# Top-k attention into a GELU block: in 18 slots POOL normalises P ahead of the next softmax's thresholds

## The chip, the core and the metric

The kernel runs on one core of a Trainium2 chip. A core has engines that work side by side, each through its own queue in order: TensorE (PE in the profile, with its weight loads as PEld), VectorE (DVE), ScalarE (ACT), GpSimd (POOL) and the queue that starts transfers (SP). An instruction that needs what another engine makes waits for a semaphore, and everything behind it in its queue waits too. The metric is the device time of one execution in microseconds.

## The reference

```python
# attention: q, k, v of (8 batches, 8 heads, 576 rows, 64)
scores = scale * np.matmul(q, k.transpose(0, 1, 3, 2))
kth = np.partition(scores, -top_k, axis=-1)[..., -top_k:-top_k + 1]   # top_k = 32
scores = np.where(scores >= kth, scores, -1e9)
attn = np.exp(scores - scores.max(axis=-1, keepdims=True))
attn = attn / (attn.sum(axis=-1, keepdims=True) + 1e-9)
attn_out = np.matmul(attn, v)
# bridge: (B,H,S,D) -> x of (4608 tokens, 512)
h = x @ w_in                                       # 512 x 2048
g = 0.5 * h * (1.0 + erf(h / sqrt(2)))
return g @ w_out                                   # 2048 x 512
```

All of it is in fp32. Each row of scores keeps its 32 largest values; the rest get no weight.

## The kernel before

**Items and slots.** The attention is cut into 144 items (`items`, `N`). A main item is one tile of 128 query rows for a pair of heads; its scores are one SBUF tile `s` of 128 x 1152, two rows of 576. A tail item collects the last 64 rows of two pairs. The main loop runs over slots `n` (0 to 147), and each slot holds one stage of each of several items: scores of item n+2, top-k of item n, softmax of item n-1, transposes of item n-2, and `attend` (P times v) of item n-3. Between those, `mlp` puts pieces of the GELU block on PE: first-layer matmuls (`l1_piece`, L673), second-layer products (`products`, L811 and L809; `even_piece`, L773 and L776). From slot 13 on the flag `few[0]` is set, and the order is that of the steady state. The schedule is manual: the order of the Python calls is the order in each engine's queue.

**What item n goes through.**

- `scores` and `last_keys`: PE makes the scores, ACT copies them scaled into `s` (L378, and L341 for the last key columns).
- `sum_up` (L413, POOL), `larger` (L406, DVE) and `smaller` (L421, POOL) split the 1152 columns of a "paired" item into lists of the larger and the smaller halves, of 128 x 576 each. `larger(n + 1)` stands at the head of slot n, and so right behind the end of `top_k(n - 1)` in DVE's queue. Items 0, 1 and 18 to 27 are not paired.
- `top_k` (DVE): rounds of MAX8 (L450) and MATCH_REPLACE8 (L453). Ahead of its very end stands `inverse(n - 1)`, the reciprocal `rden` (L482) of the previous item's softmax sum. Then come a small maximum of two lists (L465) and a reduction (L466), which give the 32nd largest value `kth`.
- `threshold` (POOL): `neg` = -kth (L475) and `bias` = kth - maximum (L476), both of 128 x 2.
- `softmax` (ACT, in the next slot, one call for each of the two rows): a steep Prelu with `neg` (L495), which pushes down everything below kth, and an Exp with `bias` (L496), whose sum is `den`. `add_small` (POOL, L488) adds 1e-9.
- `normalise` (POOL): s times rden over 128 x 1152 (L507).
- `transposes`: PE turns the normalised P: `tails`, the last columns (L527; behind two matmuls L333 that make score columns of another item), and `turn_both`, eight 128 x 128 transposes (L553). ACT copies both out (L537, L574).
- `attend`: PE multiplies by v (L615, tail items L626). ACT copies the result into `xT` (L620, L631), the input of the GELU block.

So POOL's queue at the end of slot n is `threshold(n)`, `normalise(n - 1)`, `sum_up(n + 2)`, then whatever small sums of the GELU block are due (`run_small`). DVE's queue is the end of `top_k(n)`: reciprocal of item n-1, L465, L466; then slot n+1's `larger(n + 2)`.

**Chunks.** The GELU block works on chunks of 256 tokens (or 128 for the collected tails). A chunk can start once all heads of its tokens have gone through `attend`. In the slot where `attend` finishes a chunk, PE often has no piece of the GELU block left that may run ahead of it. The loop then puts the transposes of item n-2 first (`turned`, then `tails`), and the pieces of the fresh chunk behind them:

```python
if product and n > START and done[0] < len(pieces) and pieces[done[0]][0] > ready[0]:
    if turned:
        turned()
    for piece in tr[:1]:
        piece(n + 2 if few[0] else None)
    tr, ready[0] = tr[1:], n_tok[0]
```

In every other slot pieces of the block stand ahead of the transposes.

Of the kernel before, what the change touches and what calls it, by code (L numbers as in the profile page):

```python
# [14 lines left out]
def kernel(  # L15
# [30 lines left out]
    NP = H // 2  # L46
    NM = S // P
# [151 lines left out]
    def weights_size(u):  # L199


        if u not in words:
            return
        w, first, below, d = parts(u)
        nc.scalar.activation(below, first, func=AF.Prelu, bias=high, scale=2.0**-40, alpha=2.0**40)
        nc.scalar.activation(d, below, func=AF.Prelu, bias=low, scale=2.0**59, alpha=2.0**-40)
        if on_dve(u):
            nc.vector.tensor_scalar(
                w.bitcast(i32), w.bitcast(u32), 2.0**-13, None, op0=ALU.mult
            )  # L210
        else:
            nc.scalar.activation(w.bitcast(i32), w.bitcast(u32), func=AF.Copy, scale=2.0**-13)
# [5 lines left out]
    def waits(u):  # L218

        return u == ORDER[-1]  # L220
# [3 lines left out]
    def weights_add(u):  # L224
        if u in words:
            w, _, _, d = parts(u)
            nc.gpsimd.tensor_tensor(d, d, w.bitcast(i32), op=ALU.add)
        made.add(u)


    items, starts = [], []
# [14 lines left out]
    N = len(items)  # L246
# [4 lines left out]
    few = [False]  # L251
# [106 lines left out]
    def scores(i, second=False):  # L358
        if i >= N or i in S_of:
            return  # L360
        pair, t = items[i]
        S_of[i] = s = work.tile([P, 2 * S], f32, tag="s", bufs=6, name="s")
        s_ps = pair_tile("s_ps", "l1" if second else "pr")
        if not few[0]:
            last_keys(i, bank("t_ps"))()
        if t < NM:
            q_t, kt = q_of[pair][:, t * P : (t + 1) * P], kt_of[pair]
            for e in range(2):
                rows = slice(e * D, (e + 1) * D)
                nc.tensor.matmul(  # L370
                    s_ps[:, e], lhsT=q_t[rows, :], rhs=kt[rows, 0:SM], start=True, stop=True
                )
            if i == 0:

                nc.scalar.activation(s[:, 0:SM], s_ps[:, 0], func=AF.Copy, scale=scale)
                nc.scalar.activation(s[:, S + TL :], s_ps[:, 1], func=AF.Copy, scale=scale)  # L376
                return
            nc.scalar.activation(spread(s, S + TL, SM), s_ps, func=AF.Copy, scale=scale)  # L378
        else:

            for r in range(2):
                kt = kt_of[pair + r]
                for e in range(2):
                    rows = slice(e * D, (e + 1) * D)
                    nc.tensor.matmul(
                        s_ps[half(r, e), r, :], lhsT=kt[rows, SM + P + e * TL : SM + P + (e + 1) * TL],
                        rhs=kt[rows, 0:SM], start=True, stop=True,
                    )
            s2 = s.rearrange("p (r n) -> p r n", r=2)
            nc.scalar.activation(s2[:, :, 0:SM], s_ps, func=AF.Copy, scale=scale)  # L390
# [12 lines left out]
    def larger(i):  # L403

        if paired(i):
            nc.vector.tensor_tensor(lists_of[i][:, 0], *halves_of(i), op=ALU.max)  # L406
# [63 lines left out]
    def threshold(i):  # L470

        if i < 0 or i >= N:
            return
        st = stat_of[i]
        nc.gpsimd.tensor_scalar(st["neg"], st["kth"], -1.0, None, op0=ALU.mult)  # L475
        nc.gpsimd.tensor_tensor(st["bias"], st["kth"], st["first"][:, :, 0], op=ALU.subtract)  # L476
# [13 lines left out]
    def softmax(i, e):  # L490

        if i < 0 or i >= N:
            return
        st, s = stat_of[i], row(i, e)
        nc.scalar.activation(s, s, func=AF.Prelu, bias=st["neg"][:, e : e + 1], scale=1.0, alpha=STEEP)  # L495
        nc.scalar.activation(  # L496
            s, s, func=AF.Exp, bias=st["bias"][:, e : e + 1], scale=1.0,
            accum_out=st["den"][:, e : e + 1],
        )

    def normalise(i):

        if i < 0 or i >= N:
            return
        s, r = S_of[i].rearrange("p (e n) -> p e n", e=2), stat_of[i]["rden"]
        wide = bass.AP(tensor=r.tensor, offset=r.offset, ap=[list(r.ap[0]), [1, 2], [0, S]])
        nc.gpsimd.tensor_tensor(s, s, wide, op=ALU.mult)  # L507
# [5 lines left out]
    def transposes(i):  # L513
# [43 lines left out]
        def main(e):  # L557
            tp = bank("tp")
            turn_over(tp, e)
            nc.scalar.copy(  # L560
                out=pt_now[0][:, e * NM : (e + 1) * NM, x : x + P],
                in_=tp.rearrange("p (j n) -> p j n", j=NM),
            )
# [16 lines left out]
            return [tails, lambda _: both(), turn_both]  # L580
        return [tails] + [lambda _, e=e: main(e) for e in range(2)]

    def copy_x():
        while copies:
            copies.pop()()
# [387 lines left out]
    def room_in(n):  # L973

        x = n - START - 1
        if x < 1:
            return 4
        if x >= len(sizes):
            return 0
        return sizes[x] + (1 if x % 2 == 0 else -1)  # L980
# [38 lines left out]
    for pair in range(2, n_pairs):  # L1019
        b, p = divmod(pair, NP)  # L1020
# [9 lines left out]
    for n in range(ahead):  # L1030

        left[0] = room_in(n)
        few[0] = n > START + 2
        eager[0] = n > N
        if not waits(unit_in(n)):
            weights_add(unit_in(n))
        larger(n + 1)
        for piece in squares_in.pop(n, []):
            piece()
        two = few[0] and n % 2 == 0 and n + 3 < N and items[n + 3][1] < NM  # L1040
        scores(n + 2, two)
        if two:
            scores(n + 3)
        product = attend(n - 3)
        late = n > START
        if n <= START:

            softmax(n - 1, 0)
        copy_x()
        if waits(unit_in(n)):  # L1050
            weights_size(unit_in(n))
            weights_add(unit_in(n))
        mlp(1)
        if few[0] and n % 2:
            run_gelus()
        tr = transposes(n - 2)
        turned = tr.pop() if few[0] and tr else None
# [7 lines that stand above are left out]
        if not few[0] and n > START:  # L1065
            softmax(n - 1, 0)
        mlp(1)
        if not late:
            softmax(n - 1, 1)
        if few[0]:  # L1070
            softmax(n - 1, 0)
            if n % 2:
                mlp(ODD)
        mlp(1)
        if n < START:

            keep_busy((4 if product or n == 0 else 14) * (1 if n < 5 else 2), ident)
        prep = prep_in.pop(n, [])
        if n == START + 1:

            for piece in prep:
                piece(None)
            prep = []
        if len(prep) > 1 and len(tr) == 3:
            tr, prep = tr[:1] + prep[:1] + tr[1:], prep[1:]
        now = tr[:-1]
        if few[0]:
            now, tr, prep = tr + prep[:1], [], prep[1:]
        for x, piece in enumerate(now):
            piece(n + 2 if few[0] else None)  # L1090
            if n < START and product and x == 0:
                keep_busy(5 if n < 5 else 10, ident)
            ready[0] = n_tok[0]
            if few[0] and x == 2:
                break
            mlp(1)
        ready[0] = n_tok[0]
        if late:
            softmax(n - 1, 1)
        smaller(n + 1)  # L1100
        add_small(n - 1)
        for piece in tr[-1:] + prep:
            piece(None)
            mlp(1)
        if n == 1:
            keep_busy(8, ident)

        run_gelus()
        mlp(left[0])
        run_gelus()  # L1110
        if n < N:
            top_k(n, lambda: inverse(n - 1))
        else:
            inverse(n - 1)
        threshold(n)
        normalise(n - 1)
        sum_up(n + 2)
        if n in sums_in:
            weight_sums(sums_in[n])
        run_small(6)  # L1120

        if not waits(unit_in(n + 1)):
            weights_size(unit_in(n + 1))
        for m in (n + 1, n + 2):

            if m > 2 and waits(unit_in(m)) == (m == n + 1):
                load_weights(m)
        if n < NP:
            load("v", n)
# [38 lines left out]
```

## Time and profile before

| what | us |
|---|---|
| median of 3 runs | 1556.66 (1553.4 to 1557.61) |
| profiled execution, time | 1557.3 |
| profiled execution, span | 1555.5 |
| PE busy | 1522.8 |
| DVE busy | 1330.3 |
| ACT busy | 1165.3 |
| POOL busy | 1141.5 |

The granted TensorE clock was 0.994 over the span. Rows of the profile give start, duration, engine, line, operation, what it writes and reads, and in brackets the idle time of the engine ahead of it with what ended it. Where several instructions of one line follow each other they are merged into one row with their count. The answer for one line gives the least, median and greatest duration in ns, and "who waited for it" the idle time of others that its end released, with the number of times.

### The profile page before, as it was taken

What the parts mean: (1) busy time and instruction counts of PE and PEld (TensorE: products, weight loads), DVE (VectorE), ACT (ScalarE), POOL (GpSimd) and SP (SyncE); (2) the same over time, 40 slices, a digit from 0 to 9 for tenths busy, and PEclk for the clock granted to TensorE, in tenths of its full rate; (3) what the DMA queues carried; (4) which work ended last, traced back from release to release, by engine and by line L of the source; (5) the groups of instructions that cost most, each with busy time, mean ns of one, the idle gap of its engine ahead of it and who ended that gap; (6) DMA issues with size and microseconds to landing.
All of it is one profiled execution on the core that took longest, in us unless ns stands there. A gap on an engine that the chain in (4) does not pass through costs nothing. (4 is left out here: it accounts for less than half of the span.)

```text
span 1555.5 us, 28139 instructions
## 1 busy us (share of the span) xinstructions
PE 1522.8 (98%) x9280; PEld 1199.5 (77%) x9280; DVE 1330.3 (86%) x4571; ACT 1165.3 (75%) x2050; POOL 1141.5 (73%) x1291
## 2 busy tenths in 40 slices
PE   7899999999999999999999999999999999999998
PEld 5676578877777778887777778787877777787887
DVE  8998799989999988998989997988998998988700
ACT  6998877767777777777777778777777777777720
POOL 4886567767787868777787877776788786877632
PEclk9999999999999999999999999999999999999999
DMA  6513210012101111012201111002110111000000
GB/s 180 158 61 117 89 45 1 1 37 54 24 15 31 35 26 31 1 30 42 39 18 16 30 31 45 1 23 36 34 24 22 24 30 32 15 1 15 7 14 14
DMA packets 185298, 56.35 MB, mean 36 GB/s; under 512 B 176161, under 2 KB 176705, under 8 KB 185153
## 3 DMA queue, kind: packets, MB, share of 16 engines
q1 hardware_dynamic: 183888, 54.13, 14.6%
q8 instruction: 73, 1.20, 0.3%
q14 instruction: 73, 0.59, 0.1%
q10 hardware_dynamic: 1200, 0.39, 0.1%
q0 software_dynamic: 64, 0.03, 0.0%
HBM read 45.08 MB, written 9.44 MB: 35 GB/s over the span
## 5 line engine op out<-in xcount | busy, mean ns | idle before, releaser
L673 PE MATMUL h_ps<-xT,w_in_sb 128*128 128x256 f32 (+1 forms) x2560 | 541.4, 362 | 1.9 <-ACT xT L620 1.9
L673 PEld LDWEIGHTS h_ps<-xT,w_in_sb 128*128 128x128 f32 x2560 | 435.4, 191 | 73.4 <-issue 25.3
L450 DVE MAX8 top<-lists 128x8 f32<-128x288 f32 x792 | 321.1, 447 | 0.0
L507 POOL TENSOR_TENSOR s<-s,rden 128x1152 f32<-128x1152 f32 x144 | 302.7, 2102 | 0.3 <-DVE rden L482 0.3
L496 ACT ACTIVATE s<-s,bias 128x576 f32<-128x576 f32 x288 | 223.3, 775 | 11.9
L453 DVE MATCH_REPLACE8 lists<-top,lists 128x288 f32<-128x288 f32 x528 | 229.8, 443 | 0.0
L495 ACT ACTIVATE s<-s,neg 128x576 f32<-128x576 f32 x288 | 225.7, 784 | 2.8 <-POOL neg L475 2.7
L450 DVE MAX8 low<-lists 128x8 f32<-128x288 f32 x528 | 213.1, 445 | 0.0
L574 ACT COPY pt<-tp 128x1024 f32<-128x1024 f32 x133 | 134.8, 1014 | 96.1 <-PE tp L553 96.1
L488 POOL TENSOR_SCALAR den<-den 128x2 f32<-128x2 f32 x144 | 31.4, 218 | 236.0 <-ACT s L496 232.1
L421 POOL TENSOR_TENSOR lists<-lists 128x576 int32<-128x576 int32 x132 | 186.3, 1411 | 4.0
L413 POOL TENSOR_TENSOR lists<-s 128x576 int32<-128x576 int32 x132 | 185.6, 1406 | 0.0
L553 PE MATMUL tp<-ident,s 128*128 128x128 f32 x1152 | 150.7, 274 | 7.7 <-POOL s L507 7.7
L553 PEld LDWEIGHTS tp<-ident,s 128*128 128x128 f32 x1152 | 133.7, 141 | 27.3 <-POOL s L507 14.0
L615 PE MATMUL o<-pt,raw_v 128*64 128x256 f32 x1280 | 154.1, 386 | 0.4 <-ACT pt L560 0.4
L615 PEld LDWEIGHTS o<-pt,raw_v 128*64 128x64 f32 x1280 | 86.9, 137 | 87.0 <-issue 44.7
L475 POOL TENSOR_SCALAR neg<-kth 128x2 f32<-128x2 f32 x132 | 85.6, 649 | 88.3 <-DVE kth L466 88.3
L482 DVE RECIPROCAL rden<-den 128x2 f32<-128x2 f32 x144 | 23.4, 162 | 139.8 <-POOL den L488 138.6
L811 PE MATMUL y_ps<-w_out_sb,sum 128*128 128x256 f32 x480 | 142.8, 379 | 0.0
L378 ACT ACTIVATE s<-s_ps 128x1024 f32<-128x1024 f32 x127 | 124.3, 1025 | 15.7 <-PE s_ps L370 15.5
L370 PE MATMUL s_ps<-kt,qm 64*128 64x512 f32 x512 | 131.2, 626 | 0.8 <-ACT s L376 0.8
L453 DVE MATCH_REPLACE8 lists<-low,lists 128x288 f32<-128x288 f32 x264 | 114.9, 443 | 0.0
(148 smaller groups left out, 2784.1 us busy)
## 6 DMA issues: line engine op xcount, KB each, us to landing
raw_v<-in_v_dram SPq DMA_DIRECT2D x64, 128.0 KB, 2.4
out_dram<-y SPq DMA_DIRECT2D x30, 256.0 KB, 2.1
w_out_sb<-in_moe_w_in_dram SPq DMA_DIRECT2D x14, 511.8 KB, 4.9
raw_q<-in_q_dram SPq DMA_DIRECT2D x96, 64.0 KB, 2.0
raw_k<-in_k_dram SPq DMA_DIRECT2D x96, 64.0 KB, 2.0
w_out_sb<-in_moe_w_out_dram SPq DMA_DIRECT2D x10, 511.8 KB, 4.1
w_sum<-in_moe_w_out_dram SPq DMA_DIRECT2D x6, 511.8 KB, 4.1
raw_q<-in_q_dram SPq DMA_DIRECT2D x96, 8.0 KB, 1.8
```

The costliest lines, as they stand in the source:

```text
L413: nc.gpsimd.tensor_tensor(t[:, 1].bitcast(i32), a.bitcast(i32), b.bitcast(i32), op=ALU.add)
L421: nc.gpsimd.tensor_tensor(both, both, top, op=ALU.subtract)
L450: nc.vector.max(x[:, e], src[:, e])
L453: nc.vector.match_replace(dst[:, e], x[:, e], src[:, e], LOWEST)
L495: nc.scalar.activation(s, s, func=AF.Prelu, bias=st["neg"][:, e : e + 1], scale=1.0, alpha=STEEP)
L496: nc.scalar.activation(s, s, func=AF.Exp, bias=st["bias"][:, e : e + 1], scale=1.0, accum_out=st["den"][:, e : e + 1],)
L507: nc.gpsimd.tensor_tensor(s, s, wide, op=ALU.mult)
L553: nc.tensor.transpose(tp[:, j * P : (j + 1) * P], s[:, first + j * P : first + (j + 1) * P], ident)
L574: nc.scalar.copy(out=pt_now[0][:, 0 : 2 * NM, x : x + P], in_=tp.rearrange("p e (j n) -> p (e j) n", j=NM),)
L615: nc.tensor.matmul(o[e * D : (e + 1) * D, 0:n], lhsT=vt[:, j, e, :], rhs=pt[:, e * NM + j if j < NM else 2 * NM, :], start=(j == 0), stop= ...
L673: nc.tensor.matmul(h_tile(u)[:, i, :], lhsT=w_in_sb[:, ko, f * P : (f + 1) * P], rhs=xT[:, ko, c0 : c0 + n], start=(ko == 0), stop=(ko == ...
L811: nc.tensor.matmul(acc[names][:, k], lhsT=lhsT, rhs=rhs, start=(j == 0 and k == 0), stop=(j == FT // 2 - 1 and k == 1),)
```

## The change

A helper `closes(i)` says whether `attend` of item i finishes a chunk: the last pair of heads in a batch with an odd tile, or the second of the two tail items of an odd batch. In slot n, if item n-2 is such an item (its `attend` comes in slot n+1), the two calls at the end of the slot change places: `normalise(n - 1)` goes on POOL's queue first, `threshold(n)` behind it. In all other slots nothing changes.

```diff
+    def closes(i):
+        if i < 0 or i >= N:
+            return False
+        pair, t = items[i]
+        b, at = divmod(pair, NP)
+        return at == NP - 1 and t % 2 == 1 if t < NM else at == NP - 2 and b % 2 == 1
...
-        threshold(n)
-        normalise(n - 1)
+        if few[0] and closes(n - 2):
+            normalise(n - 1)
+            threshold(n)
+        else:
+            threshold(n)
+            normalise(n - 1)
         sum_up(n + 2)
```

The slots are 17, 21, 29, 37, 45, 53, 57, 65, 73, 81, 89, 93, 101, 109, 117, 125, 129 and 137; 145 is selected as well, but there is neither a threshold nor a further item in it. In 21, 57, 93 and 129 the chunk finished is one of 128 tail tokens.

## The prediction

> **What bounds the kernel now.** I read the page's busy shares first, then the answer for the line that normalises P (L507), then the timeline around the slots the change touches, engine by engine.
>
> ```profile
> PE 1522.8 (98%) x9280; PEld 1199.5 (77%) x9280; DVE 1330.3 (86%) x4571; ACT 1165.3 (75%) x2050; POOL 1141.5 (73%) x1291
> ...
> L507 POOL TENSOR_TENSOR s<-s,rden x144: 2097/2102/2108, 30.5 to 1479.4; 128x1152 f32<-128x1152 f32 x144
> ...
>   PE tp L553: 7.7, 13
> ...
>   PE tp_t L527: 0.5, 3
> ```
>
> PE is busy 98% of the span, so only its gaps can be won. The row of L553, under "who waited for it", is the prize: in 13 places PE's large transposes (L553) waited for the normalised P, 7.7 us together. No edit of this kind can bring more than that, 0.5% of the span. One place, slot 45 and what follows it, row by row:
>
> ```profile
> 478.15 0.15 DVE L482 RECIPROCAL rden<-den 128x2 f32<-128x2 f32 x1
> 478.27 0.19 DVE L465 TENSOR_TENSOR top<-top,low 128x32 f32<-128x32 f32 x1
> 478.60 0.75 DVE L406 TENSOR_TENSOR lists<-s 128x576 f32<-128x576 f32 x1
> 478.76 0.66 POOL L475 TENSOR_SCALAR neg<-kth 128x2 f32<-128x2 f32 x1 [1.20 <-DVE kth L466]
> 479.54 2.10 POOL L507 TENSOR_TENSOR s<-s,rden 128x1152 f32<-128x1152 f32 x1
> 481.69 1.09 PE L553 MATMUL tp<-ident,s 128*128 128x128 f32 x8 [1.09 <-POOL s L507]
> 488.27 0.17 DVE L482 RECIPROCAL rden<-den 128x2 f32<-128x2 f32 x1 [0.40 <-POOL den L488]
> 489.61 2.10 POOL L507 TENSOR_TENSOR s<-s,rden 128x1152 f32<-128x1152 f32 x1
> 493.54 0.27 PE L527 MATMUL tp_t<-ident,s 128*128 128x128 f32 x1
> ```
>
> The reciprocal that L507 needs is ready at 478.30, but POOL first waits for kth, makes neg and bias, and starts L507 at 479.54. It ends at 481.64 and PE, idle for 1.09, starts 0.05 later.
>
> **The change part by part.** No instruction is added or removed on any engine; PE, DVE, ACT and SP keep their order. In POOL's queue L507 moves ahead of L475 and L476 in 18 slots: 17, 21, 29, 37, 45, 53, 57, 65, 73, 81, 89, 93, 101, 109, 117, 125, 129 and 137 (slot 145 is chosen too, but has no threshold). So it stops waiting for kth and queues only behind the reciprocal.
>
> *What L507 gains.* In slot 45 POOL started 0.08 after the reduce of kth ended (the row of neg), so I start L507 0.08 after the reciprocal, at 478.38 instead of 479.54. That is 1.16 earlier, or 1.1 if the little maximum L465 holds it a moment. The largest of the 13 waits is 1.09, so all of them go: minus 7.7 us if nothing is late in exchange.
>
> *What neg and bias lose.* They now stand behind 2.10 us of L507, and end some 2 us later. The softmax on ACT waits for neg. In an ordinary closing slot ACT reaches that softmax only after copies that wait for the same transposes, so I cost this at nothing there; without that cover it would cost ACT up to 2 us a slot. In three slots (57, 93, 129; after the next fence) ACT goes straight to it, and is costed below. POOL's next operation, the sum L413, starts no later than now, since POOL no longer idles for kth.
>
> *What the early L507 meets.* Now it starts after the two-input maximum L406 of DVE has begun and soon finished; after the change it is in flight when L406 wants to start. The trace shows what such pairs do to POOL:
>
> ```profile
> L475 POOL TENSOR_SCALAR neg<-kth x132: 217/658/662, 38.6 to 1471.1; 128x2 f32<-128x2 f32 x132
> L475 POOL TENSOR_SCALAR neg<-top x12: 218/219/789, 19.3 to 297.5; 128x2 f32<-128x2 f32 x12
> ...
> 286.97 0.22 POOL L475 TENSOR_SCALAR neg<-top 128x2 f32<-128x2 f32 x1
> 287.01 0.76 DVE L406 TENSOR_TENSOR lists<-s 128x576 f32<-128x576 f32 x1
> 287.15 0.67 POOL L476 TENSOR_TENSOR bias<-top,first 128x2 f32<-128x2 f32 x1
> ```
>
> The same neg takes 0.22 us alone and 0.66 where it starts behind L406: in slot 45 it ends at 479.42, 0.07 after L406 (479.35). POOL is held until DVE's instruction is over. The bias at 287.15 shows it again, ending 0.05 after L406. The other order, POOL in flight and L406 coming, stands only once, at 286.97, with a neg of two columns, and neither was held. So how long L406 is held by a 2.10 us L507 is not shown. Its lower bound is 0 (that one row). Its upper bound is the rest of L507: 478.38 + 2.10 + 0.07 - 478.60 = 1.95, or 2.05 where L406 comes 0.39 instead of 0.45 after the reciprocal, as it does in most slots. I take 2.05: the rows nearest in kind, where two long readers really overlap, all show the second held to the end of the first, while the lone neg reads two columns and may have read them before L406 asked. The Trainium skill, "SBUF — State Buffer", section "Who interferes with whom", says that a VectorE instruction with two SBUF inputs and a GpSimd instruction that reads SBUF exclude each other, whoever starts first having the port for its whole instruction; the trace agrees for VectorE first, and by the rule the hold here would be those 2 us, by the lone row nothing.
>
> *What 2.05 us on DVE costs.* L406 heads the next item's top-k, so DVE's reciprocal one slot later is late by 2.05 less the time it already waits there. L507 of that slot (not swapped) is late by as much, and PE reads it first with the small transpose L527, two slots on. In slot 45's case: 2.05 - 0.40 = 1.65 late; L507 ended 491.71 and PE came at 493.54, a margin of 1.78 after the 0.05 hand-over. The net is margin minus lateness, 0.13 won of 1.09; the other 0.96 is a new wait of PE. Slots 81 and 117 repeat slot 45: 3 x 0.13 = 0.39. The other families:
>
> ```profile
> 197.50 1.09 PE L553 MATMUL tp<-ident,s 128*128 128x128 f32 x8 [0.22 <-POOL s L507]
> ...
> 327.20 0.17 DVE L482 RECIPROCAL rden<-den 128x2 f32<-128x2 f32 x1
> 328.53 2.10 POOL L507 TENSOR_TENSOR s<-s,rden 128x1152 f32<-128x1152 f32 x1
> 332.72 0.27 PE L527 MATMUL tp_t<-ident,s 128*128 128x128 f32 x1
> ...
> 407.99 0.17 DVE L482 RECIPROCAL rden<-den 128x2 f32<-128x2 f32 x1 [0.46 <-POOL den L488]
> 409.32 2.10 POOL L507 TENSOR_TENSOR s<-s,rden 128x1152 f32<-128x1152 f32 x1
> 413.26 0.27 PE L527 MATMUL tp_t<-ident,s 128*128 128x128 f32 x1
> ...
> 563.25 1.09 PE L553 MATMUL tp<-ident,s 128*128 128x128 f32 x8 [0.49 <-POOL s L507]
> 570.07 0.17 DVE L482 RECIPROCAL rden<-den 128x2 f32<-128x2 f32 x1 [1.43 <-POOL den L488]
> 571.40 2.10 POOL L507 TENSOR_TENSOR s<-s,rden 128x1152 f32<-128x1152 f32 x1
> 577.80 1.04 PE L553 MATMUL tp<-ident,s 128*128 128x128 f32 x8
> ```
>
> - Slot 17: its next-but-one item takes no paired top-k, so there is no L406 to hold. Won: 0.22.
> - Slots 29, 65, 101: the reciprocal's row shows no wait, so 2.05 stays; margin 332.72 - 330.63 - 0.05 = 2.04. Net 0.0.
> - Slots 37, 73, 109: 2.05 - 0.46 = 1.59; margin 413.26 - 411.42 - 0.05 = 1.79. Won: 3 x 0.20 = 0.6.
> - Slots 53, 89, 125: 2.05 - 1.43 = 0.62 late; PE comes 4.3 after L507, and its small transpose about 1 before that. Won in full: 3 x 0.49 = 1.47.
> - Slots 21 and 137: no wait to win.
>
> ```profile
> 604.01 0.17 DVE L482 RECIPROCAL rden<-den 128x2 f32<-128x2 f32 x1 [1.72 <-POOL den L488]
> 604.40 0.75 DVE L406 TENSOR_TENSOR lists<-s 128x576 f32<-128x576 f32 x1
> 605.25 0.78 ACT L495 ACTIVATE s<-s,neg 128x576 f32<-128x576 f32 x1 [0.52 <-POOL neg L475]
> 605.34 2.10 POOL L507 TENSOR_TENSOR s<-s,rden 128x1152 f32<-128x1152 f32 x1
> 607.86 0.28 ACT L341 ACTIVATE s<-tp_t 128x128 f32<-128x128 f32 x1 [0.88 <-PE tp_t L527]
> 609.60 1.01 ACT L574 COPY pt<-tp 128x1024 f32<-128x1024 f32 x1 [1.31 <-PE tp L553]
> 613.38 0.17 DVE L482 RECIPROCAL rden<-den 128x2 f32<-128x2 f32 x1 [0.49 <-POOL den L488]
> 614.72 2.10 POOL L507 TENSOR_TENSOR s<-s,rden 128x1152 f32<-128x1152 f32 x1
> 616.87 0.33 PE L527 MATMUL tp_t<-ident,s 128*128 128x128 f32 x1 [0.18 <-POOL s L507]
> ```
>
> - Slots 57, 93, 129 finish the 128-token chunk. L553 does not wait there, so nothing is won. The softmax at 605.25 already waits for neg and comes about 2 us later; ACT's own waits behind it, 0.88 and 1.31, take up 2.19, so its copies end on time. But DVE is late by 2.05 - 0.49 = 1.56, and the next L507 has no margin: PE already waits 0.18 for it at 616.87. Lost: 3 x 1.56 = 4.68.
>
> *The sum:* 0.39 + 0.22 + 0.0 + 0.6 + 1.47 - 4.68 = -2.0, so 2.0 us longer. Against the profiled execution (span 1555.5, time 1557.3) that is 1559.3; that execution lies 0.6 above the median of 1556.66, so I predict 1558.7, 0.13% slower. A measurement of this kernel can tell about 0.3% (4.7 us) from no change, so this is "no change" on the slow side.
>
> **The rivals.**
>
> *Nothing is held* (hold 0). For it: the row at 286.97. Against it: 0.66 where 0.22 would do, on POOL. All 7.7 us are won: 1549.0, faster.
>
> *DVE goes first whenever it comes*: L406 passes the running L507, which stops for 0.75 + 0.07. For it: in every overlap shown, POOL was the one held, and never DVE. In slot 45 L507 then ends at 478.38 + 2.10 + 0.82 = 481.30, 0.3 earlier than now instead of 1.1, and DVE loses nothing: 12 x 0.3 + 0.2 = 3.8 won, 1552.9. That is also the case where the change doesn't do what it says.
>
> *POOL keeps the port* (the other side). When L507 ends, neg and bias are next in POOL's queue and read too. If they go before the waiting L406, it is held for two more operations of 0.22: 2.49. Nine places (29, 65, 101; 37, 73, 109; 45, 81, 117) and the three of the tail chunk then lose 0.44 more each, 12 x 0.44 = 5.3, so 7.3 in all: 1564.0. If the sum behind them went first too it would be worse. Against it: L406 asked long before neg. It decides from a hold of about 2.27 us on, since the sum moves 12 us per us of hold, and 2.7 more reaches 0.3%.
>
> **How the numbers follow.** Held to the end of L507: 0.56. Nothing held: 0.16. DVE first: 0.12. POOL keeps the port: 0.16. The predicted time is that of the first, 1558.7. The range 1548.5 to 1563 takes in the first three and leaves out most of the fourth. Faster by over 0.3% is the second case and a little more, 0.17; slower is the fourth and the upper edge of the first, where some margins are only 0.1 us wide, 0.19; within 0.3%: 0.64.
>
> **What would show it.** In the changed profile L507 of slots 29 to 129 should start under 0.2 us after its reciprocal, and "PE tp L553" under L507's waiters should fall from 7.7 towards 0. If L406 is held, its row in those slots is some 2.8 us long or starts 2 us later, and "PE tp_t L527" under L507's waiters rises from 0.5 to about 8 us, with waits of about 1.7 us after slots 57, 93 and 129. If L406 stays at 0.75 and L507 at 2.10 in those slots, nothing was held; an L507 of 2.9 us means that DVE goes first. I am wrong most easily in the hold: each 0.1 us of it moves the sum by 1.2 us.

## The result, and the profile after

The changed kernel takes 1561.24 us (median of 8 runs, 1557.15 to 1562.24), the kernel before 1555.54 in the same comparison (8 runs, 1553.03 to 1558.11). The ratio is 1.0032, with an interval of 1.0021 to 1.0044: some 5 us slower by the ratio, while the two medians are 5.7 apart. The profiled execution after has a span of 1559.8 us, against 1555.5.

The page's busy line and the answer for L507 of the changed kernel, with those who waited for it:

```profile
PE 1524.9 (98%) x9280; PEld 1199.7 (77%) x9280; DVE 1360.2 (87%) x4571; ACT 1167.5 (75%) x2050; POOL 1144.1 (73%) x1291
...
L507 POOL TENSOR_TENSOR s<-s,rden x144: 2101/2103/2110, 30.6 to 1483.7; 128x1152 f32<-128x1152 f32 x144
...
  PEld tp_t L527: 15.3, 25
  PE tp_t L527: 10.4, 16
  PEld tp L553: 1.6, 4
```

PE no longer waits for L507 with its large transposes L553: the 7.7 us are gone. In their place it waits 10.4 us with the small transpose L527, which was 0.5 before. DVE is busy 30 us longer with the same instructions, the mark of something held. The timeline of the changed kernel around slot 45, DVE, POOL and PE, shows both ends:

```profile
478.03 0.15 DVE L482 RECIPROCAL rden<-den 128x2 f32<-128x2 f32 x1
478.26 2.11 POOL L507 TENSOR_TENSOR s<-s,rden 128x1152 f32<-128x1152 f32 x1 [0.82 <-DVE rden L482]
478.48 2.50 DVE L406 TENSOR_TENSOR lists<-s 128x576 f32<-128x576 f32 x1
480.34 0.72 POOL L475 TENSOR_SCALAR neg<-kth 128x2 f32<-128x2 f32 x1
480.43 1.09 PE L553 MATMUL tp<-ident,s 128*128 128x128 f32 x8
481.58 0.27 PE L527 MATMUL tp_t<-ident,s 128*128 128x128 f32 x1
489.45 0.13 DVE L482 RECIPROCAL rden<-den 128x2 f32<-128x2 f32 x1
490.05 0.66 POOL L475 TENSOR_SCALAR neg<-kth 128x2 f32<-128x2 f32 x1 [2.23 <-DVE kth L466]
490.83 2.10 POOL L507 TENSOR_TENSOR s<-s,rden 128x1152 f32<-128x1152 f32 x1
492.98 0.33 PE L527 MATMUL tp_t<-ident,s 128*128 128x128 f32 x1 [0.55 <-POOL s L507]
...
503.85 0.27 PE L527 MATMUL tp_t<-ident,s 128*128 128x128 f32 x1
513.33 0.33 PE L527 MATMUL tp_t<-ident,s 128*128 128x128 f32 x1 [0.34 <-POOL s L507]
523.99 0.33 PE L527 MATMUL tp_t<-ident,s 128*128 128x128 f32 x1 [0.36 <-POOL s L507]
```

L507 starts 0.08 after the reciprocal and PE starts L553 without a wait. But L406 takes 2.50 us instead of 0.75, and one slot later the reciprocal comes at 489.45 instead of 488.27. kth, neg and the next L507 follow it, and PE waits 0.55, and again 0.34 and 0.36 four and five slots behind the exchange. The same small transposes in the kernel before:

```profile
482.85 0.27 PE L527 MATMUL tp_t<-ident,s 128*128 128x128 f32 x1
...
504.35 0.27 PE L527 MATMUL tp_t<-ident,s 128*128 128x128 f32 x1
513.33 0.27 PE L527 MATMUL tp_t<-ident,s 128*128 128x128 f32 x1
523.50 0.33 PE L527 MATMUL tp_t<-ident,s 128*128 128x128 f32 x1
```

PE ran 1.27 ahead of the kernel before at 481.58 (0.13 of that from earlier slots), 0.56 ahead at 492.98 (493.54 before), 0.50 ahead at 503.85, level at 513.33 and 0.49 behind at 523.99. Such differences of the same instruction in two traces I call PE's shift; they resolve 0.02 us per slot, where the times of whole runs spread by 5 us. Taken at L553 over the whole kernel (the shift seven slots on minus the shift at the exchange; four for slots 53, 57 and their like), they give this, plus meaning time lost:

| exchanged slots | predicted, us | changed kernel, us |
|---|---|---|
| 17 | -0.22 | -0.29 |
| 29, 65, 101 | 0.0 | -0.39, -0.35, -0.36 (-1.1 together) |
| 37, 73, 109 | -0.60 together | +0.47, +0.49, +0.47 (+1.4 together) |
| 45, 81, 117 | -0.39 together | +0.62, +0.59, +0.59 (+1.8 together) |
| 53, 89, 125 | -1.47 together | -0.55 each (-1.7 together) |
| 57, 93, 129 (128 tail tokens) | +4.68 together | +1.33, +1.35, +1.35 (+4.0 together) |
| sum, slot 16 to 143 | +2.0 | +4.3 |

The waits for L507 alone add up to less: 10.4 - 0.5 - 7.7 = 2.2 us more than before. The other 2.1 us the page books as PE's busy time (1524.9 against 1522.8): in 16 places where L527 is late, it starts up to 0.16 us later behind L333 than its bracket counts. PE's shift has both.

### The profile page after: what moved, and what is told of

The parts are those of the page before. It is cut to its first block, busy times and chain, and to the rows that moved or that the text cites. A ratio compares the mean times of both kernels' runs of the same rounds, so it can differ in the third digit from the quotient of the medians.

```text
span 1559.8 us, 28141 instructions
## 1 busy us (share of the span) xinstructions
PE 1524.9 (98%) x9280; PEld 1199.7 (77%) x9280; DVE 1360.2 (87%) x4571; ACT 1167.5 (75%) x2050; POOL 1144.1 (73%) x1291
## 4 chain that ended last, share of the span: by engine, by line
PE 61%; DVE 13%; POOL 11%; issue 2%; ACT 2%; DVEq 0%; POOLq 0%
PE h_ps L681 22%; PE y_ps L819 13%; PE o L623 6%; PE tp L553 5%; PE s_ps L370 5%; DVE lists L453 4%; POOL s L507 3%; DVE top L450 3%; PE seven L817 2%; DVE low L450 2%; PE y_ps L781 1%; PE y_ps L784 1%; POOL lists L413 1%; POOL lists L421 1%; PE o L634 1%
## 5 line engine op out<-in xcount | busy, mean ns | idle before, releaser
L507 POOL TENSOR_TENSOR s<-s,rden 128x1152 f32<-128x1152 f32 x144 | 303.0, 2104 | 9.3 <-DVE rden L482 6.1
L495 ACT ACTIVATE s<-s,neg 128x576 f32<-128x576 f32 x288 | 225.1, 782 | 16.9 <-POOL neg L475 16.4
L413 POOL TENSOR_TENSOR lists<-s 128x576 int32<-128x576 int32 x132 | 185.9, 1409 | 0.0
L553 PE MATMUL tp<-ident,s 128*128 128x128 f32 x1152 | 150.9, 274 | 0.0
L553 PEld LDWEIGHTS tp<-ident,s 128*128 128x128 f32 x1152 | 133.8, 141 | 18.8 <-issue 4.6
L406 DVE TENSOR_TENSOR lists<-s 128x576 f32<-128x576 f32 x132 | 127.7, 968 | 0.0
```

The lines of the kernel that those rows point to most:

```text
L413: nc.gpsimd.tensor_tensor(t[:, 1].bitcast(i32), a.bitcast(i32), b.bitcast(i32), op=ALU.add)
L553: nc.tensor.transpose(tp[:, j * P : (j + 1) * P], s[:, first + j * P : first + (j + 1) * P], ident)
```

## The experiments

Theory A is that the cost is the hold of L406 behind L507. Theory B is that it is the late neg and bias. All kernels start from the changed one unless said otherwise.

**The maximum later.** L507 stays early. In the slot behind an exchange, the first round of the next top-k (MAX8 and MATCH_REPLACE8) goes ahead of L406:

```diff
+        if n - 1 > START + 2 and closes(n - 3) and n < N and paired(n + 1):
+            begun[n] = top_k_parts(n, lambda: inverse(n - 1))
+            next(begun[n])
         larger(n + 1)
...
+    begun = {}
     def top_k(i, last):
+        for _ in begun.pop(i, None) or top_k_parts(i, last):
+            pass
+    def top_k_parts(i, last):
...
             if r == len(rounds) - 1:
                 last()
+            if r == 0:
+                yield
```

> Theory A (the port): the change costs time because L406, two inputs on DVE, is held about 1.8 us behind the running L507, and the lateness of DVE comes back as waits of PE. Here L507 is early as in the changed kernel, but in those slots L406 stands behind the first round of the next top-k (two MAX8, two MATCH_REPLACE8, 1.57 us of one-input work), so that L507 is nearly over when it comes. A expects L406 at 0.75 to 1.2 us in every slot, PE's waits for L507 back to under 1 us, and the whole 7.7 us won against the kernel before: ratio 0.995. Theory B (the late thresholds): neg and bias, 2 us later than before, are what costs. They stay just as late here, so B expects a ratio of 1.003 as in the changed kernel.

Measured: 1548.65 us (1545.78 to 1548.83, 5 runs) against 1556.2, ratio 0.9946 (0.9934 to 0.9958). The lines moved down by 8: L515 is the normalisation, L483 neg, L561 and L535 PE's transposes. Its timeline around slot 45, and who waited for L515:

```profile
474.07 2.11 POOL L515 TENSOR_TENSOR s<-s,rden 128x1152 f32<-128x1152 f32 x1 [0.81 <-DVE rden L490]
475.87 0.93 DVE L406 TENSOR_TENSOR lists<-s 128x576 f32<-128x576 f32 x1
476.15 0.72 POOL L483 TENSOR_SCALAR neg<-kth 128x2 f32<-128x2 f32 x1
476.24 1.09 PE L561 MATMUL tp<-ident,s 128*128 128x128 f32 x8
...
  PE tp_t L535: 0.7, 3
```

L406 is held for 0.2 us (0.25 at most), neg is as late behind the reciprocal as in the changed kernel, and the waits are gone. B falls. PE's shift is -8.8 us from slot 16 to 143, a little more than the 7.7 of the waits; 0.2 us in each of the slots 57, 93 and 129 come from no wait of L553. This version beats both kernels.

**Parts of the change alone.** First the seven slots in which the changed profile gains, then the three tail slots:

```diff
-        if few[0] and closes(n - 2):
+        if n in (17, 29, 53, 65, 89, 101, 125):
```

> The exchange only in slots 17, 29, 53, 65, 89, 101 and 125, where PE's clockwork of the changed profile runs ahead of that of before by 0.29, 0.39, 0.55, 0.35, 0.55, 0.36 and 0.55 us, 3.0 us together. If the slots act one by one (theory A with its slot table), this kernel is 3.0 us shorter than before: ratio 0.998. If a gain in one slot only widens the wait in a later one, it is between 0 and 2 us: ratio 0.999 to 1.000.

```diff
-        if few[0] and closes(n - 2):
+        if n in (57, 93, 129):
```

> The exchange only in slots 57, 93 and 129, which finish 128 tail tokens. The changed profile loses 1.33, 1.36 and 1.35 us around them. If the slots act one by one: 4.0 us longer than before, ratio 1.0026, with three waits of PE's L527 of 1.8 us. If the loss there hangs on the exchanges of the slots ahead: under 1 us, ratio 1.000.

Measured: 1551.54 us, ratio 0.9969 (0.9957 to 0.9981), and 1561.24 us, ratio 1.0032 (1.0020 to 1.0044). Both intervals hold the expected 0.998 and 1.0026. PE's shift is sharper: -3.00 us for the first, as expected, and +4.04 for the second. With the tail slots alone, PE waits just where it does in the changed kernel:

```profile
617.39 0.33 PE L527 MATMUL tp_t<-ident,s 128*128 128x128 f32 x1 [1.80 <-POOL s L507]
```

So the slots act one by one. What the six slots 37, 45, 73, 81, 109 and 117 lose is then the rest: 4.26 + 3.00 - 4.04 = 3.2 us.

**L507 in two halves.** If the hold is one instruction long, a shorter instruction holds less:

```diff
-    def normalise(i):
+    def normalise(i, cut=False):
...
+        if cut:
+            for e in range(2):
+                nc.gpsimd.tensor_tensor(s[:, e], s[:, e], wide[:, e], op=ALU.mult)
+            return
         nc.gpsimd.tensor_tensor(s, s, wide, op=ALU.mult)
...
         if few[0] and closes(n - 2):
-            normalise(n - 1)
+            normalise(n - 1, True)
             threshold(n)
```

> As the changed kernel, but in the exchanged slots L507 is two instructions of one row of 576 each, about 1.07 us. If the port is kept for a whole instruction and then goes to the one that waits, L406 gets in after the first half: its row is about 1.6 us instead of 2.5, the second half's row is about 1.07 + 0.7, and the pair ends 0.8 later than one L507. DVE's lateness halves to 0.9: the slots 37 to 117 lose nothing more, the tail slots lose about 0.4 each, and the waits won shrink to 0.3 each: ratio 0.998 to 1.000. If POOL keeps the port as long as it has work, L406 stays at 2.5 us and the ratio at 1.003.

Measured: 1550.46 us, ratio 0.9963 (0.9952 to 0.9975), better than expected. The timeline around slot 45, where the two halves stand in one row (L509), and the answer for that line:

```profile
476.96 2.76 POOL L509 TENSOR_TENSOR s<-s,rden 128x576 f32<-128x576 f32 x2 [0.81 <-DVE rden L482]
477.18 1.54 DVE L406 TENSOR_TENSOR lists<-s 128x576 f32<-128x576 f32 x1
479.11 1.33 PE L557 MATMUL tp<-ident,s 128*128 128x128 f32 x8
...
L509 POOL TENSOR_TENSOR s<-s,rden x36: 1145/1148/1663, 194.5 to 1408.2; 128x576 f32<-128x576 f32 x36
```

L406 gets in after the first half (1.54, at most 1.62 in any slot), and the second half, held in turn, takes 1.66 instead of 1.15. So the one that waits is served at the next instruction's end, also when POOL has more work queued. What I had overlooked is that PE's first transposes read only the first half: they start at 479.11, 0.6 ahead of the pair's end (476.96 + 2.76 = 479.72), and PE's matmuls are not among those who waited for L509. That goes with the better ratio; PE's shift is -5.1 us.

**Where the lateness survives.** Theory C: around slots 37, 45 and their like, DVE's lateness goes on for three slots more because the reciprocal's wait for POOL's den is no slack: POOL's queue ahead of den is itself full from the late kth on. Theory D: it goes through ACT's softmax. Two of POOL's sums of y are left out in six slots, in the changed kernel and in the one before; a part of the output is then not y.

```diff
+        if n in (39, 47, 75, 83, 111, 119):
+            del small[:2]
+            run_small(4)
+        else:
+            run_small(6)
-        run_small(6)
```

> The changed kernel, with two of POOL's sums of the output (0.73 us each) left out in each of slots 39, 47, 75, 83, 111 and 119, two slots behind an exchange, so a part of y is wrong. Theory C: around slots 37, 45, 73, 81, 109 and 117 the lateness of DVE lives on because the reciprocal three slots on waits for POOL's den, and POOL's queue ahead of den is full from the late kth on; DVE's wait there is no slack. With 1.45 us less in that queue the lateness of about 1.05 us ends there, the second waits (0.6 and 0.23, or 0.55 and 0.43 us per place) go, and of the 4.3 us of loss about 5 are won back: ratio to before 0.999 to 1.000. Theory D, that the lateness comes through ACT's softmax: the two sums change nothing, ratio 1.003.

> The kernel before with the same twelve sums left out: the control. C and D expect 0.0 us, ratio 1.000: without an exchange PE waits for nothing that hangs on POOL's queue in those slots.

Measured: 1553.91 us, ratio 0.9990 (0.9981 to 1.0000) for the changed kernel without these sums, 1556.03 us, ratio 1.0002 (0.9992 to 1.0013) for the control. C holds. In PE's shift the changed kernel goes from +4.26 to -1.38: 5.6 us won back, where 5 were expected, and the six slots now gain 0.37 to 0.40 each. The control moves by 0.4, 0.35 of it in one odd wait at slot 90: there a transfer of q landed late, and DVE stood 1.59 us for it ahead of L270 (0.0 in the kernel before). The rows that carry it, POOL and DVE behind slot 37 of the changed kernel:

```profile
418.96 0.66 POOL L475 TENSOR_SCALAR neg<-kth 128x2 f32<-128x2 f32 x1 [1.72 <-DVE kth L466]
...
426.71 0.74 POOL L869 TENSOR_TENSOR y<-y 128x256 f32<-128x256 f32 x1
427.40 1.41 POOL L421 TENSOR_TENSOR lists<-lists 128x576 int32<-128x576 int32 x1
428.89 0.22 POOL L488 TENSOR_SCALAR den<-den 128x2 f32<-128x2 f32 x1
429.15 0.17 DVE L482 RECIPROCAL rden<-den 128x2 f32<-128x2 f32 x1 [1.86 <-POOL den L488]
```

The same of the kernel before, and of the changed kernel without the two sums:

```profile
418.83 0.66 POOL L475 TENSOR_SCALAR neg<-kth 128x2 f32<-128x2 f32 x1 [0.59 <-DVE kth L466]
...
427.27 1.41 POOL L421 TENSOR_TENSOR lists<-lists 128x576 int32<-128x576 int32 x1
428.79 0.22 POOL L488 TENSOR_SCALAR den<-den 128x2 f32<-128x2 f32 x1
429.04 0.17 DVE L482 RECIPROCAL rden<-den 128x2 f32<-128x2 f32 x1 [1.89 <-POOL den L488]
```

```profile
423.50 1.40 POOL L421 TENSOR_TENSOR lists<-lists 128x576 int32<-128x576 int32 x1
425.31 0.22 POOL L488 TENSOR_SCALAR den<-den 128x2 f32<-128x2 f32 x1 [0.40 <-ACT s L496]
425.56 0.17 DVE L482 RECIPROCAL rden<-den 128x2 f32<-128x2 f32 x1 [0.79 <-POOL den L488]
```

In the changed kernel no row of POOL behind neg at 418.96, up to den at 428.89, bears an idle time. In the kernel before it is the same from 418.83 to 428.79, so the full queue could be read there before the change; there it cost nothing, as the control shows. PE runs 0.95 ahead of the kernel before (423.12 against 424.07 at L527), but den does not: 428.89 against 428.79. DVE's 1.86 us of idling there looks like slack, and is the end of a loop: kth, neg, the full queue, den, and DVE again. With 1.45 us less in the queue, den waits for ACT instead (0.40), in step with PE. The six slots gain although ACT still waits for neg as before (14.8 us in 14 places, 16.4 in 14 in the changed kernel), so D falls.

**The later maximum alone.** The first experiment's place of L406, with POOL's order as in the kernel before; the lines are shown against the first experiment:

```diff
-        if few[0] and closes(n - 2):
-            normalise(n - 1)
-            threshold(n)
-        else:
-            threshold(n)
-            normalise(n - 1)
+        threshold(n)
+        normalise(n - 1)
```

> Only the later place of L406 from the run with the late maximum; L507 stays behind neg and bias in all slots. neg is no longer held by L406 (0.22 instead of 0.66), so L507 starts 0.44 us earlier and up to 0.44 of each wait is won, about 4.5 us over the 13 waits; but L406 now comes when L507 has about 0.9 us to go and is held for that, which costs the three tail slots about 0.4 us each and the slots 37 to 117 little. Ratio 0.997 to 0.998. If the order on POOL were what wins in that run, and not the place of L406, the ratio is 1.000.

Measured: 1552.58 us, ratio 0.9978 (0.9969 to 0.9988), as expected. Its timeline around slot 45:

```profile
475.23 0.22 POOL L483 TENSOR_SCALAR neg<-kth 128x2 f32<-128x2 f32 x1 [1.20 <-DVE kth L474]
476.63 1.64 DVE L406 TENSOR_TENSOR lists<-s 128x576 f32<-128x576 f32 x1
477.62 1.93 POOL L413 TENSOR_TENSOR lists<-s 128x576 int32<-128x576 int32 x1
```

neg takes 0.22 again, L406 is held for 0.9 behind L507, and POOL's next reader L413 for 0.5 behind L406. So the best kernel needs both: the order on POOL and the place of L406.

## Why the prediction was right or wrong

The range of 1548.5 to 1563 holds the time, and the sign of the point is right. The size is not: 2.0 us were forecast, and 4.3 (PE's shift), 5 (the ratio) or 5.7 (the medians) measured, just past the 0.3% that I called no change. That the total came this close is partly luck, as two errors of opposite sign stand in it.

- *What L507 gains*: right. It starts 0.08 after the reciprocal (0.15 in slot 17), and all 13 waits of L553 are gone. The prize was a little larger than the 7.7: in the tail slots the weight load of L527 waited 0.27 for L507 too, and PE now starts it 0.30 earlier.
- *What neg and bias lose*: right. They are about 2 us late and cost nothing. ACT waits for neg 2.4 us in each of the slots 57, 93 and 129, and its copies still do not hold PE up; with the later maximum, where they are as late, the kernel is at its fastest.
- *What the early L507 meets*: right in kind, and the rival "nothing is held" is out. The term was mis-sized: L406 is held for 1.75 to 1.83 us, not 2.05, since it ends only 0.61 after L507 and not 0.75 + 0.07. Its rows gave 1.95 for slots like 45 and about 2.02 for the others, while 2.05 was used for all. By my own rate of 12 us per us of hold the difference is 2.6 to 3.6 us to the good. The Trainium skill, "SBUF — State Buffer", section "Who interferes with whom", has the port go to whoever starts first for the whole instruction; L406 at 2.50 to 2.58 behind L507, and at 1.54 to 1.62 behind half of it, agrees.
- *What it costs on DVE, one slot on*: right as a mechanism. PE's L527 waits where it was said to, in slots 57, 93 and 129 too: a loss of 1.56 each was forecast, 1.33 to 1.35 measured, by the shorter hold. (The wait itself grows by 1.63, from 0.18 to 1.81, since PE arrives 0.30 earlier.) These rows of the changed kernel are the counterpart of the last ones shown before it:

```profile
604.34 2.58 DVE L406 TENSOR_TENSOR lists<-s 128x576 f32<-128x576 f32 x1
614.60 0.14 DVE L482 RECIPROCAL rden<-den 128x2 f32<-128x2 f32 x1
615.98 2.10 POOL L507 TENSOR_TENSOR s<-s,rden 128x1152 f32<-128x1152 f32 x1
618.14 0.33 PE L527 MATMUL tp_t<-ident,s 128*128 128x128 f32 x1 [1.81 <-POOL s L507]
```

- *The step that failed* is the sum for slots 37, 73, 109 and 45, 81, 117: -1.0 forecast, +3.2 measured. I ended their account at the first L527 after the exchange. The lateness that was left, about 1 us, was to be nothing because the reciprocal idles later; the experiment on POOL's sums shows that this idling is the loop's own. The waits there cost over 5 us (5.6 came back without the two sums), and the over-sized hold hid half of the error in the total.
- The rival *POOL keeps the port* has a time nearly as close to the measured one as mine, 1564.0, and is wrong: neg ends behind L406 in every exchanged slot that has one (480.34 + 0.72 = 481.06, L406 480.98), and L406 got in between the two halves. *DVE goes first* is wrong as well: L507 stays at 2.10 to 2.11.

## What to carry to other kernels

Before an instruction is moved, look at what the other engine of the same port will be doing at the new place; here the cure was to move the other one as well, by one round of work that does not use the port. An idle time ended by another engine is slack only if that engine idled too: follow its rows back, and if they stand without a gap to something that your own lateness delays, the wait moves with it. Where runs spread by 5 us, compare the start of the same instructions in two traces slot by slot; here that added up to some hundredths of a us, and told gains from losses that cancel.

## What the runs showed of the hardware

The hold took a second VectorE instruction that I had not counted. Behind slot 17 there is no L406, but a scaling of weights with one input (L208) stands in its place; the first row is the changed kernel's, the second that of the kernel before:

```profile
194.54 2.59 DVE L208 TENSOR_SCALAR w_sum<-w_sum 128x1024 int32<-128x1024 uint32 x1
```

```profile
194.48 0.69 DVE L208 TENSOR_SCALAR w_sum<-w_sum 128x1024 int32<-128x1024 uint32 x1
```

It was held for 1.9 us. The MAX8 and MATCH_REPLACE8 rows, 0.44 us each, ran at their usual times beside L507.

The spread between runs of one kernel stands in two places. In the profiles of the experiments, PE's transposes of slot 16 stand between 3.0 us earlier and 0.2 us later than in the kernel before. From there to slot 143 the clockwork of unchanged slots agrees to 0.02 us, but for the one late transfer of the control. Behind slot 143 three profiles (the two halves, the control and the later maximum alone) win another 1.7 us. The granted clock goes with both. From 106 to 120 us it is 0.88 in the kernel before and in the four profiles that start like it or up to 0.8 earlier, and the rows that the kernel before has between 110.5 and 115 us take 4.06 us. In the four that are 2.5 us ahead or more it is 1.00, and the same rows take 2.39. At the end, rows that the kernel before has between 1543 and 1549 us take 5.46 against 3.77 us, with a clock of 0.95 to 0.96 from 1490 us on against 0.97 to 0.98. Why the clock was granted differently was not tried.
